# u's products over four token tiles at a time, GELU stores a piece later, two more x tiles kept in DRAM

## The chip, the cores and the metric

One NeuronCore of a Trainium2 chip runs the kernel. The metric is device microseconds of one execution; the kernel before has a median of 753.14 us over three runs (752.85 to 754.17).

## The reference

With x of 2048 tokens by D = 640, the output is a gated mix of two layers.

```python
g = sigmoid((x * gate_w).sum(-1))
a = Re(DFT_seq @ (x @ DFT_hid))          # Cr @ (x Dr^T) - Ci @ (x Di^T)
q = x @ w_q                               # 32 heads x 2 halves of 128
s1, s2 = q1 @ k1.T, q2 @ k2.T             # 16 keys each
top_e, top_s = best 2 of the 4 sums of the best 2 of s1 and of s2
act = gelu(x @ u[top_e])                  # u: 256 experts x 640
b = sum over heads and k of softmax(top_s) * act * v[top_e]
out = g * a + (1 - g) * b
```

All 256 products x @ u.T are computed for every token, and the chosen ones are weighted afterwards. "u's products" are these: 256 experts by 2048 tokens, contracted over 640, then GELU.

## The kernel before

Every product is made in a three-matmul form: both operands are split into a high and a low part (a ScalarE copy makes the high part, a subtraction on VectorE or GpSimd the low one), and `mm3` (L141) issues high x high, high x low and low x high into one accumulator bank.

**Pieces.** The backbone is `seq_piece(n)` (L229) for n = 0 to 127: the product of one 128 x 512 piece of the sequence DFT with one x tile, 5 x 3 matmuls of 512 columns into banks 0 to 4. 16 pieces make a piece sum q, which ScalarE copies into the five buffers ST (L246), VectorE multiplies by the gate (`gate_piece`) and a DMA stores (`store_piece`, L221, on ScalarE's queue). A piece's data is loaded five pieces ahead and split three pieces ahead (`load_piece`, `split_piece`). After the pieces a tail of 2 x 42 steps multiplies the sums by the hidden DFT and by v.

**The order is written by hand.** `at(n, f)` (L196) hangs f behind piece n; `follow(n)` (L199) runs what hangs there, in the order in which it was hung. "Place 24" below is what hangs behind piece 24. Each engine and each DMA queue (SP's, ScalarE's, GpSimd's) executes its share of this one order in sequence and waits at the first thing that isn't ready. VectorE's search for the best keys (`topk`, `gates`, `weights`) comes in small portions: `run_bg` gives them a credit for each TensorE stretch, so they are spread over the pieces. `weights` (L669) is a batch of four tiles' softmax, `put_rows` (L695) copies its transposed rows on ScalarE (L697).

**First phase, pieces 0 to 29.** All 16 x tiles are split and kept in SBUF (X0 to X15). Beside the pieces, `w_part` (L358) multiplies w_q with the keys in eight groups G, at places 6, 9, ..., 27: 32 matmuls (L365) on four tiles of wq (`load_wq`, 640 KB each, five buffers, on SP's queue, at the places between). `make_t` forms sums of the results. As later stages need the space, `put_x` (L449) stores X0 to X8 to DRAM (AWAY = 9) at places 6 to 22; `get_x` (L452) brings tiles back when a later round of 16 pieces needs them, through X6 to X8 in turn. The five stores of piece sum 0 hang at place 24. u is loaded and split at places 21 to 27 (`load_u`, `split_u`), the first token pair's xT at place 26 (`split_xT`, xh on ScalarE, xl on GpSimd), its sums at place 28 (`sum_xT`, L429, VectorE).

**Second phase, pieces 30 to 65.** Beside the pieces run eight score steps p = 0 to 7 (two token tiles each) in four parts a = 0 to 3, one part a place (`score_step`, L544), with one free piece ahead of steps 2, 4 and 6 ("free": nothing of a score step hangs at it). Part 0 multiplies into bank A (two mm3), has ScalarE split four sums of xT (`split_sums_xT`, L443), runs `u_pair` (L720) and copies A to Z on ScalarE (L548). Part 1 goes on in Z (three mm3), copies it out, and makes products Y (bank 6), then Z again. Parts 2 and 3 finish the scores of the two tiles and hang the search for their best keys into the background; part 3 ends with `sum_xT` of the next pair on VectorE. `u_pair(p)` makes u's products of its two tiles: 2 x 5 mm3 with 256 moving columns (two tiles of 128) into bank 7, one GELU of 128 x 512 (L729), and two stores of 128 KB by SP, all within part 0.

**Third phase.** From N1 = 66 on, the background goes on with the search and builds the experts' weights; `load_dd` and `split_dd` bring the hidden DFT. For the tail, buffers of x tiles are lent out again in the order of `raw_tags` (L950).

Of the kernel before, what the change touches and what calls it, by code (L numbers as in the profile page):

```python
# [38 lines left out]
KZ = KD + 1  # L39
NSTEP = 7 * KZ  # L40
AHEAD = 5
AWAY = 9
BYPASS = 4
ACCUM_END = NT * (NC + 2) - 4

# [61 lines left out]
def gated_mix_kernel(ctx: ExitStack, tc: tile.TileContext, xT, xn, dreT, dimT, wsre, wsim, wq, kT, uT, vv, gw, out):  # L107
# [20 lines left out]
    def ps_t(shape, dt=F32):  # L128
        return bank(7, shape, dt)
# [6 lines left out]
    def split(f, h, l, eng):  # L136

        nc.scalar.activation(h, f, AF.Copy)  # L138
        eng.tensor_sub(l, f, h.bitcast(F32))  # L139
# [15 lines left out]
    def run_bg(us):  # L155
        bg.run(us, share)
# [39 lines left out]
    def at(n, f, *args):  # L196
        then.setdefault(n, []).append(lambda: f(*args))
# [51 lines left out]
    for q in range(2 * NC):  # L249
        n = NT * (q + 1)  # L250
        at(n + (2 if q == 0 else -2 if q > 1 else -1), load_row, q)
        at(n + (7 if q == 0 else 0), gate_piece, q)
        if q in (1, 2, 3, 4):
            for d in range(KD):
                at(n + 1 + d, store_piece, q, (d,))
        else:
            at(n + (8 if q == 0 else 1), store_piece, q)


    p1_stack = ctx.enter_context(ExitStack())  # L260
    p1 = p1_stack.enter_context(tc.tile_pool(name="p1", bufs=1, reuse_waits="tile"))
    pools = [p1]

    def load_x(s):
        if s < NT:
# [4 lines left out]
    def split_x(s):  # L270

        if s < NT:
            X[s] = big.tile([P, 2, D], F32R, name="X", tag=f"X{s}")
            f = xr[s // 2][:, s % 2]
            if s:
                split(f, X[s][:, 0], X[s][:, 1], nc.vector)
                return
            psp[0] = h, l = WS[:, 0, 0], WS[:, 0, 1]
            a, b, w = slice(0, 2 * P), slice(2 * P, D), pf.pop(0)
            nc.vector.tensor_copy(X[0][:, 0, a], f[:, a])  # L280
            nc.scalar.activation(h, w, AF.Copy)
            nc.scalar.activation(X[0][:, 0, b], f[:, b], AF.Copy)
            nc.vector.tensor_sub(l, w, h.bitcast(F32))
            for c in (a, b):
                nc.vector.tensor_sub(X[0][:, 1, c], f[:, c], X[0][:, 0, c].bitcast(F32))
# [20 lines left out]


    warm = nc.const_aps.tensor(1.0, [P, 2 * P], mybir.dt.bfloat16)
    t = ps_t([P, 2 * P])
    for n in range(WARM):  # L310
        nc.tensor.matmul(t, warm[:, :P], warm, start=True, stop=True)  # L311

    split_x(0)
    load_piece(4)
# [105 lines left out]
    def split_xT(p, n):  # L420

        if p < NP:
            if not xs:
                xs.update((t, big.tile([P, 2, KD, P], F32R, name=t, tag=t)) for t in ("xh", "xl"))
            split(xf[p][:, n], xs["xh"][:, n], xs["xl"][:, n], nc.gpsimd)

    SX = {}

# [21 lines left out]
        nc.sync.dma_start(xd[s], X[s].bitcast(F32))  # L450

    def get_x(s, tag):  # L452
        X[s] = big.tile([P, 2, D], F32R, name="X", tag=f"X{tag}")
        nc.sync.dma_start(X[s].bitcast(F32), xd[s])

    for s in range(AWAY):
        at(6 + 2 * s, put_x, s)
    for s in range(3):
        at(2 * NT - 5 + s, get_x, s, 6 + s)
    for n in range(NT - 4):  # L460
        at(n, load_x, n + 4)
    for n in range(NT - 3):
# [6 lines left out]
    for G in range(NG):  # L469
        b = 6 + 3 * G  # L470
        for m in range(4 * G, 4 * G + 4):
            at(b, w_part, m)
        at(b, split_w, G)
        if G >= NG // 2:
            at(b + (4, 3, 2, 1)[G - NG // 2], make_t, G)
        for i, m in enumerate(range(4 * G + WQB, 4 * G + WQB + 4)):
            at(b + i // 2, load_wq, m)
    n = b + 2
    at(n - 8, load_xT, 0)
    for k in range(KD):  # L480
        at(n - 8 + k, load_u, k)
        at(n - 6 + k, split_u, k)
    for a in range(2):
        at(n - 3, split_xT, 0, a)
    at(n - 1, sum_xT, 0)
    assert N0 == n + 1

# [34 lines left out]
    def products(o, *terms, first=False):  # L522


        terms = [t for a, w in terms for t in zip(*a, *w)]
        for n, (ah, al, wh, wl) in enumerate(terms):
            mm3(o, ah, al, wh, wl, first and n == 0, n == len(terms) - 1, True)
            run_bg(0.68)

    def x_part(n, k0, k1):  # L530
        return [[xs[t][:, n, k] for k in range(k0, k1)] for t in ("xh", "xl")]

    def s_part(n):
        return [[t[:, k * P:(k + 1) * P] for k in range(2)] for t in SX[n]]

    def w_part2(k0, k1, c):
        return [[w[:, k, c * TC:(c + 1) * TC] for k in range(k0, k1)] for w in (WH, WL)]

    def t_part(n):
        return [[w[:, k] for k in range(2)] for w in TW[n]]  # L540
# [3 lines left out]
    def score_step(p, a):  # L544


        i0, i1 = 2 * p, 2 * p + 1
        copy = lambda o, f: nc.scalar.activation(o, f, AF.Copy)  # L548
        if a == 0:
            AB["A"] = bank(5)  # L550
            products(AB["A"], (x_part(0, 0, 2), w_part2(0, 2, 0)), first=True)
            split_sums_xT(p)
            u_pair(p)
            AB["Z"] = bank(7)
            copy(AB["Z"], AB["A"])
        elif a == 1:
            products(AB["Z"], (x_part(0, 2, 4), w_part2(2, 4, 0)), (x_part(0, 4, 5), w_part2(4, 5, 0)))
            new_sc(i0)
            copy(sc_half(i0, 0), AB["Z"])
            AB["Y"] = bank(6)  # L560
            products(AB["Y"], (s_part(1), t_part(1)), first=True)
            AB["Z"] = bank(7)
            copy(AB["Z"], AB["Y"])
            load_xT(p + 1)
        elif a == 2:
            products(AB["A"], (s_part(2), t_part(2)))
            copy(sc_half(i0, 1), AB["A"])
            products(AB["Z"], (s_part(4), w_part2(2, 4, 1)), (x_part(0, 4, 5), w_part2(4, 5, 1)))
            nc.vector.tensor_add(sc_half(i0, 1), sc_half(i0, 1), AB["Z"])
            bg.credit -= 0.75  # L570
            picks(i0, scs.pop(i0))
            products(AB["A"], (s_part(3), t_part(3)))
            new_sc(i1)
            copy(sc_half(i1, 1), AB["A"])
            split_xT(p + 1, 0)
        else:
            products(AB["Y"], (x_part(1, 4, 5), w_part2(4, 5, 1)))
            nc.vector.tensor_add(sc_half(i1, 1), sc_half(i1, 1), AB["Y"])
            products(AB["A"], (x_part(1, 2, 4), t_part(4)), (x_part(1, 4, 5), w_part2(4, 5, 0)))
            copy(sc_half(i1, 0), AB["A"])  # L580
            bg.credit -= 0.75
            picks(i1, scs.pop(i1))
            split_xT(p + 1, 1)
            sum_xT(p + 1)
# [132 lines left out]
        if i % NB == NB - 1:  # L717
            bg.add(gates(i // NB))

    def u_pair(p):  # L720
        xh, xl = xs["xh"], xs["xl"]
        ps = bank(7, (P, 2, 2 * P))
        for n in range(2):
            c = slice(n * P, (n + 1) * P)
            for k in range(KD):
                mm3(ps[:, n, :], UH[:, k, c], UL[:, k, c], xh[:, :, k, :], xl[:, :, k, :], k == 0 and n == 0, k == KD - 1, True)
            run_bg(1.8)
        act = p2.tile([P, 2, 2 * P], F32, name="act")
        nc.scalar.activation(act, ps, AF.Gelu_apprx_tanh)  # L729
        for n in range(2):  # L730
            nc.sync.dma_start(actd[n][:, 2 * p * P:2 * (p + 1) * P], act[:, n])

    for p in range(NP):
        n = N0 + 4 * p + p // 2
        for a in range(4):
            at(n + 1 + a, score_step, p, a)
    N1 = n + 5
# [3 lines left out]
            at(n - (3 if s > 2 else 5), get_x, s, 6 + s % 3)  # L741
    for s in range(3, AWAY):
        at(N1 - 5 + s, get_x, s, s)
    for s in range(3):
        at(N1 + 6 + 3 * s, get_x, s, s)

# [116 lines left out]
            draw.pop(m)  # L863

    for m in range(2):
        at(N1 + 4 + 2 * m, load_dd, m)
    for m in range(KD):
        for a in range(2):
            at(N1 + 6 + 5 * m + 2 * a, split_dd, m, a)
# [44 lines left out]
    def split_sums(k):  # L914
        if k == KD:
            f = p3.tile([P, 4 * TC], F32R, name="ts", tag="hot0")
            TS[8] = f[:, :2 * D]
            raw_free.append(f[:, 2 * D:2 * D + TC].bitcast(F32))
            raw_tags.extend((("xf", 2), ("X9", 2)))
        for n in () if k == KD else [k] + ([5 + k // 2] if k % 2 == 0 else []):  # L920
            TS[n] = big.tile([P, 2 * D], F32R, name="ts", tag=f"X{(1, 3, 4, 5, 6, 0, 2, 7)[n]}")
        t = T["t"]
        t1, t5, t3, t6 = (t[:, n * 2 * P:(n + 1) * 2 * P] for n in range(4))
        for n, f in enumerate((t1, t3, t5, t6, t[:, 8 * P:])):
            split(f, t_sum(k, n, 0), t_sum(k, n, 1), nc.gpsimd if n < 2 else nc.vector)
        bg.credit -= 1.0

    def load_v():
        T[KD] = big.tile([P, 2, D], F32, name="dt", tag="X9")
        nc.sync.dma_start(T[KD], vv.rearrange("k p d -> p k d"))  # L930

    def split_v():
# [13 lines left out]
    at(NPC + 14, store_gates, 1)  # L946


    fresh, raw_free = deque(), deque()
    raw_tags = [("X8", 2)] + [("wf", 1)] * 4 + [("X10", 2), ("wf", 1)] + [(f"X{s}", 2) for s in range(11, 16)]  # L950
    raw, sp = {}, {}

    def take(key):
# [305 lines left out]
```

## Time and profile before

| | |
|---|---|
| median of three runs | 753.14 us |
| the profiled execution's own time | 753.44 us |
| its span, first to last instruction | 751.7 us |
| DMA moved | 165.89 MB, mean 221 GB/s |
| granted TensorE clock | 1.0 throughout |

A page of the profile gives each engine's busy time, the span in 40 slices (18.8 us each; a digit is a busy share in tenths), the DMA queues, the chain of work that ended last, the costliest groups and the DMA issues. Views of the trace add the timeline of an engine (start, length, engine, line, operation, output<-inputs, shape, count, and in brackets the idle time before it with what ended it), sums by windows, and the chain in order of time. A matmul's length in the timeline reaches into the next one; the distance between starts is what it costs.

### The profile page before, as it was taken

The numbers are of one execution on the slowest core, as the hardware profiler recorded it, in microseconds if no ns is written. First come the engines' busy times: TensorE is split into PE (matmuls) and PEld (weight loads), VectorE is DVE, ScalarE is ACT, GpSimd is POOL, SyncE is SP. The second block draws the span as 40 slices with busy tenths as digits, with TensorE's granted clock in tenths as the row PEclk, the third lists the DMA queues.
The fourth block names the chain that finished last, engine by engine and source line by source line (L and its number), as shares of the span: only waits on it lengthen the run. The fifth ranks groups of instructions, "written<-read, shape, count | busy, mean of one in ns | idle before, by whom it ended". The sixth has DMA issues, their size and how long they took to land.

```text
span 751.7 us, 11366 instructions
## 1 busy us (share of the span) xinstructions
PE 746.7 (99%) x4045; PEld 610.7 (81%) x4045; DVE 587.4 (78%) x741; ACT 361.7 (48%) x660; POOL 346.6 (46%) x286
## 2 busy tenths in 40 slices
PE   9999999999999999999999999999999999999998
PEld 7777777888888888888888888888888888888887
DVE  6864088278999999998999888979999983357651
ACT  4334134534345835553734687633555653443451
POOL 5533225342424424334345445643356793487253
PEclk9999999999999999999999999999999999999999
DMA  9999999478366786663496856388766689775301
GB/s 334 378 388 356 342 381 345 132 191 278 57 174 149 184 273 164 159 167 118 121 376 210 175 146 203 116 255 291 264 225 209 218 261 335 228 233 182 112 29 71
DMA packets 84490, 165.89 MB, mean 221 GB/s; under 512 B 16081, under 2 KB 23377, under 8 KB 84177
## 3 DMA queue, kind: packets, MB, share of 16 engines
q1 hardware_dynamic: 70960, 140.89, 55.5%
q0 software_dynamic: 5472, 9.96, 8.6%
q10 hardware_dynamic: 8000, 14.31, 5.2%
q8 instruction: 32, 0.52, 0.3%
q14 instruction: 26, 0.20, 0.1%
HBM read 132.46 MB, written 31.08 MB: 218 GB/s over the span
## 4 chain that ended last, share of the span: by engine, by line
PE 96%; DMA 2%; DVE 2%; issue 0%; SPq 0%; ACT 0%
PE b L143 30%; PE b L144 30%; PE b L145 30%; PE b L239 2%; PE b L365 2%; DMA wq<-in_wq 2%; PE b L815 1%; PE b L311 1%; DVE ST L217 1%; DVE WU L139 0%; DVE tw L139 0%; DVE wp L371 0%; ACT WU L138 0%; DVE tt L397 0%; DVE tt L396 0%
## 5 line engine op out<-in xcount | busy, mean ns | idle before, releaser
L143 PE MATMUL b<-WS,X 128*128 128x512 f32 x620 | 243.5, 393 | 0.0
L144 PE MATMUL b<-WS,X 128*128 128x512 f32 x620 | 241.5, 389 | 0.0
L145 PE MATMUL b<-WS,X 128*128 128x512 f32 x620 | 241.3, 389 | 0.0
L139 POOL TENSOR_TENSOR WS<-wf,WS 128x512 fp32r<-128x512 f32 x89 | 135.9, 1532 | 162.8 <-ACT WS L138 157.9
L143 PEld LDWEIGHTS b<-WS,X 128*128 128x128 f32 x620 | 116.4, 188 | 28.0 <-issue 4.1
L145 PEld LDWEIGHTS b<-WS,X 128*128 128x128 f32 x620 | 116.4, 188 | 24.5
L144 PEld LDWEIGHTS b<-WS,X 128*128 128x128 f32 x620 | 116.4, 188 | 23.3
L138 ACT ACTIVATE WS<-wf 128x512 fp32r<-128x512 f32 x89 | 55.7, 629 | 76.9 <-PE b L145 32.1
L803 DVE TENSOR_TENSOR hot<-rows,wtab 128x1024 f16<-128x1024 f16 x64 | 62.7, 1005 | 0.7 <-PE b L815 0.6
L139 POOL TENSOR_TENSOR WS<-ra,WS 128x512 fp32r<-128x512 f32 x39 | 55.1, 1426 | 15.3 <-ACT WS L138 13.2
L139 POOL TENSOR_TENSOR xl<-xf,xh 128x640 fp32r<-128x640 f32 x16 | 28.2, 1767 | 69.3 <-ACT xh L138 62.9
L138 ACT ACTIVATE WS<-ra 128x512 fp32r<-128x512 f32 x55 | 34.5, 631 | 50.9 <-PE b L145 36.0
L548 ACT ACTIVATE sc<-b 128x512 f32<-128x512 f32 x32 | 19.2, 600 | 80.7 <-PE b L145 80.7
L191 POOL DMA_DIRECT2D WS<-in_wsre x30 | 26.4, 880 | 68.0 <-ACT WS L189 66.6
L773 ACT ACTIVATE b<-b,mask 128x128 f32<-128x128 f32 x128 | 43.0, 342 | 13.5 <-PE b L815 10.4
L139 POOL TENSOR_TENSOR WP<-ra,WP 128x512 fp32r<-128x512 f32 x18 | 26.4, 1482 | 43.2 <-ACT WP L138 43.1
L598 DVE TENSOR_TENSOR eq<-sc,mm 128x1024 f16<-128x1024 f32 x32 | 41.4, 1293 | 0.9
L605 DVE TENSOR_REDUCE tied<-eq 128x64 f32<-128x1024 f16 x32 | 39.0, 1219 | 0.9
L596 DVE TENSOR_REDUCE mm<-sc 128x64 f32<-128x1024 f32 x32 | 38.8, 1212 | 0.3
L217 DVE SCALAR_TENSOR_TENSOR ST<-ST,grow 128x512 f32<-128x512 f32 x40 | 31.4, 846 | 0.6 <-ACT ST L246 0.6
L143 PE MATMUL b<-WU,xh 128*128 128x512 f32 x80 | 31.2, 391 | 0.0
L145 PE MATMUL b<-WU,xl 128*128 128x512 f32 x80 | 31.1, 389 | 0.0
(203 smaller groups left out, 1468.8 us busy)
## 6 DMA issues: line engine op xcount, KB each, us to landing
wq<-in_wq SPq DMA_DIRECT2D x32, 640.0 KB, 7.1
X<-xd SPq DMA_DIRECT2D x30, 640.0 KB, 6.6
wf<-in_wsim SPq DMA_DIRECT2D x64, 256.0 KB, 4.8
wf<-in_wsre SPq DMA_DIRECT2D x63, 256.0 KB, 6.5
ra<-pd SPq DMA_DIRECT2D x47, 256.0 KB, 3.7
pd<-ST ACTq DMA_DIRECT2D x35, 256.0 KB, 5.2
WS<-in_wsre POOLq DMA_DIRECT2D x30, 256.0 KB, 5.3
xd<-X SPq DMA_DIRECT2D x9, 640.0 KB, 9.4
```

What stands on the lines that cost most here:

```text
L138: nc.scalar.activation(h, f, AF.Copy)
L139: eng.tensor_sub(l, f, h.bitcast(F32))
L143: nc.tensor.matmul(o, wh, ah, start=first, stop=False, skip_group_check=more)
L144: nc.tensor.matmul(o, wh, al, start=False, stop=False, skip_group_check=more)
L145: nc.tensor.matmul(o, wl, ah, start=False, stop=last, skip_group_check=more)
L191: nc.gpsimd.dma_start(l, (wsre, wsim)[w][c, s], accum_op=OP.add)
L217: nc.vector.scalar_tensor_tensor(f, f, -1.0 if w else 1.0, g, op0=OP.mult, op1=OP.mult)
L596: nc.vector.tensor_reduce(m, sc, op=OP.max, axis=AX.X)
L598: nc.vector.tensor_tensor(eq, sc, m[:, :, None].to_broadcast([P, HH, E]), op=OP.is_equal)
L605: nc.vector.tensor_reduce(tied[:, s, ib, :], eq, op=OP.add, axis=AX.X)
L773: nc.scalar.activation(f[:, :, n], f[:, :, n], AF.Copy, scale=mask4[:, n:n + 1])
L803: nc.vector.tensor_tensor(o, a, b, op=op)
```

## The change

u's products are made once for two score steps, in part 0 of the odd ones: 2 x 5 mm3 with 512 moving columns (four tiles), expert half 0 into bank 7 and half 1 into bank 6. GELU of half 0 follows at once; SP stores it in part 1 (256 KB), where GELU of half 1 follows into the same buffer; that is stored in part 2. For this the split xT of two pairs is kept, in the space of X9 and X10 (xh) and of X11 and X12 (xl). X9 and X10 are therefore stored too (AWAY = 11), at place 25 behind the last load of wq, and come back like the others; X11 and X12 are copied by ScalarE into the old places of xh and xl at places 16 and 17, and back at N1. The free piece stands ahead of steps 1, 3 and 5; N1 stays 66. Piece sum 0 is stored at place 28, the first xT split at place 27, the first two load_dd one and two places later. The last warm-up matmul writes the other half of its bank. In the tail v's raw tile takes the first half of the space of X9 and X10, and what is lent out is cut anew: as many buffers, in another order.

```diff
 AHEAD = 5
-AWAY = 9
+AWAY = 11
 BYPASS = 4
...
         else:
-            at(n + (8 if q == 0 else 1), store_piece, q)
+            at(n + (12 if q == 0 else 1), store_piece, q)
     p1_stack = ctx.enter_context(ExitStack())
...
     pools = [p1]
+    TWIN = {}
+    def place(tag):
+        if tag in (9, 11):
+            TWIN[tag] = big.tile([P, 2, 2, D], F32R, name="X", tag=f"X{tag}")
+        if tag in (9, 10, 11, 12):
+            return TWIN[tag - (tag + 1) % 2][:, (tag + 1) % 2]
+        return big.tile([P, 2, D], F32R, name="X", tag=f"X{tag}" if isinstance(tag, int) else tag)
+    def move_x(s, tag):
+        old, X[s] = X[s], place(tag)
+        nc.scalar.activation(X[s], old.bitcast(F32), AF.Copy)
     def load_x(s):
...
         if s < NT:
-            X[s] = big.tile([P, 2, D], F32R, name="X", tag=f"X{s}")
+            X[s] = place(s)
             f = xr[s // 2][:, s % 2]
...
     warm = nc.const_aps.tensor(1.0, [P, 2 * P], mybir.dt.bfloat16)
-    t = ps_t([P, 2 * P])
+    t = ps_t([P, TC])
     for n in range(WARM):
-        nc.tensor.matmul(t, warm[:, :P], warm, start=True, stop=True)
+        c = slice(0, 2 * P) if n < WARM - 1 else slice(2 * P, TC)
+        nc.tensor.matmul(t[:, c], warm[:, :P], warm, start=n < WARM - 1, stop=True, skip_group_check=n == WARM - 1)
     split_x(0)
...
             if not xs:
-                xs.update((t, big.tile([P, 2, KD, P], F32R, name=t, tag=t)) for t in ("xh", "xl"))
-            split(xf[p][:, n], xs["xh"][:, n], xs["xl"][:, n], nc.gpsimd)
+                xs.update((t, big.tile([P, 2, 2, KD, P], F32R, name=t, tag=tag)) for t, tag in (("xh", "X9"), ("xl", "X11")))
+            split(xf[p][:, n], xs["xh"][:, p % 2, n], xs["xl"][:, p % 2, n], nc.gpsimd)
     SX = {}
...
     def get_x(s, tag):
-        X[s] = big.tile([P, 2, D], F32R, name="X", tag=f"X{tag}")
+        X[s] = place(tag)
         nc.sync.dma_start(X[s].bitcast(F32), xd[s])
-    for s in range(AWAY):
+    for s in range(9):
         at(6 + 2 * s, put_x, s)
...
         at(2 * NT - 5 + s, get_x, s, 6 + s)
+    for s, tag in ((11, "xh"), (12, "xl")):
+        at(s + 5, move_x, s, tag)
     for n in range(NT - 4):
...
             at(b + i // 2, load_wq, m)
+    for s in range(9, AWAY):
+        at(b - 2, put_x, s)
     n = b + 2
...
     for a in range(2):
-        at(n - 3, split_xT, 0, a)
+        at(n - 2, split_xT, 0, a)
     at(n - 1, sum_xT, 0)
...
             run_bg(0.68)
-    def x_part(n, k0, k1):
-        return [[xs[t][:, n, k] for k in range(k0, k1)] for t in ("xh", "xl")]
+    def x_part(p, n, k0, k1):
+        return [[xs[t][:, p % 2, n, k] for k in range(k0, k1)] for t in ("xh", "xl")]
     def s_part(n):
...
             AB["A"] = bank(5)
-            products(AB["A"], (x_part(0, 0, 2), w_part2(0, 2, 0)), first=True)
+            products(AB["A"], (x_part(p, 0, 0, 2), w_part2(0, 2, 0)), first=True)
             split_sums_xT(p)
-            u_pair(p)
+            if p % 2:
+                u_pairs(p // 2)
             AB["Z"] = bank(7)
...
         elif a == 1:
-            products(AB["Z"], (x_part(0, 2, 4), w_part2(2, 4, 0)), (x_part(0, 4, 5), w_part2(4, 5, 0)))
+            if p % 2:
+                store_act(p, 0)
+                put_act(1)
+            products(AB["Z"], (x_part(p, 0, 2, 4), w_part2(2, 4, 0)), (x_part(p, 0, 4, 5), w_part2(4, 5, 0)))
             new_sc(i0)
...
         elif a == 2:
+            if p % 2:
+                store_act(p, 1)
             products(AB["A"], (s_part(2), t_part(2)))
             copy(sc_half(i0, 1), AB["A"])
-            products(AB["Z"], (s_part(4), w_part2(2, 4, 1)), (x_part(0, 4, 5), w_part2(4, 5, 1)))
+            products(AB["Z"], (s_part(4), w_part2(2, 4, 1)), (x_part(p, 0, 4, 5), w_part2(4, 5, 1)))
             nc.vector.tensor_add(sc_half(i0, 1), sc_half(i0, 1), AB["Z"])
...
         else:
-            products(AB["Y"], (x_part(1, 4, 5), w_part2(4, 5, 1)))
+            products(AB["Y"], (x_part(p, 1, 4, 5), w_part2(4, 5, 1)))
             nc.vector.tensor_add(sc_half(i1, 1), sc_half(i1, 1), AB["Y"])
-            products(AB["A"], (x_part(1, 2, 4), t_part(4)), (x_part(1, 4, 5), w_part2(4, 5, 0)))
+            products(AB["A"], (x_part(p, 1, 2, 4), t_part(4)), (x_part(p, 1, 4, 5), w_part2(4, 5, 0)))
             copy(sc_half(i1, 0), AB["A"])
...
             bg.add(gates(i // NB))
-    def u_pair(p):
+    def put_act(n):
+        AB["act"] = f = p2.tile([P, TC], F32, name="act")
+        nc.scalar.activation(f, AB.pop(("u", n)), AF.Gelu_apprx_tanh)
+    def store_act(p, n):
+        nc.sync.dma_start(actd[n][:, p // 2 * TC:(p // 2 + 1) * TC], AB.pop("act"))
+    def u_pairs(c):
         xh, xl = xs["xh"], xs["xl"]
-        ps = bank(7, (P, 2, 2 * P))
         for n in range(2):
-            c = slice(n * P, (n + 1) * P)
+            e = slice(n * P, (n + 1) * P)
+            AB["u", n] = ps = bank(7 - n)
             for k in range(KD):
-                mm3(ps[:, n, :], UH[:, k, c], UL[:, k, c], xh[:, :, k, :], xl[:, :, k, :], k == 0 and n == 0, k == KD - 1, True)
-            run_bg(1.8)
-        act = p2.tile([P, 2, 2 * P], F32, name="act")
-        nc.scalar.activation(act, ps, AF.Gelu_apprx_tanh)
-        for n in range(2):
-            nc.sync.dma_start(actd[n][:, 2 * p * P:2 * (p + 1) * P], act[:, n])
+                mm3(ps, UH[:, k, e], UL[:, k, e], xh[:, :, :, k, :], xl[:, :, :, k, :], k == 0, k == KD - 1)
+                run_bg(0.68)
+            if n == 0:
+                put_act(0)
     for p in range(NP):
-        n = N0 + 4 * p + p // 2
+        n = N0 + 4 * p + min((p + 1) // 2, 3)
         for a in range(4):
...
         at(N1 - 5 + s, get_x, s, s)
+    for s in (11, 12):
+        at(N1, move_x, s, s)
     for s in range(3):
...
     for m in range(2):
-        at(N1 + 4 + 2 * m, load_dd, m)
+        at(N1 + 5 + 3 * m, load_dd, m)
     for m in range(KD):
...
             TS[8] = f[:, :2 * D]
-            raw_free.append(f[:, 2 * D:2 * D + TC].bitcast(F32))
-            raw_tags.extend((("xf", 2), ("X9", 2)))
+            raw_free.extend(LENT[0][:, a * TC:(a + 1) * TC] for a in range(2))
+            raw_tags.append(("xf", 2))
         for n in () if k == KD else [k] + ([5 + k // 2] if k % 2 == 0 else []):
...
     def load_v():
-        T[KD] = big.tile([P, 2, D], F32, name="dt", tag="X9")
+        f = big.tile([P, 2, 2, D], F32, name="dt", tag="X9")
+        T[KD], f = f[:, 0], f[:, 1].rearrange("p k d -> p (k d)")
+        fresh.extend(f[:, a * TC:(a + 1) * TC] for a in range(2))
+        LENT.append(T[KD].rearrange("p k d -> p (k d)"))
         nc.sync.dma_start(T[KD], vv.rearrange("k p d -> p k d"))
...
     at(NPC + 14, store_gates, 1)
-    fresh, raw_free = deque(), deque()
-    raw_tags = [("X8", 2)] + [("wf", 1)] * 4 + [("X10", 2), ("wf", 1)] + [(f"X{s}", 2) for s in range(11, 16)]
+    LENT, fresh, raw_free = [], deque(), deque()
+    raw_tags = [("X8", 2)] + [("wf", 1)] * 5 + [("X11", 5)] + [(f"X{s}", 2) for s in range(13, 16)]
     raw, sp = {}, {}
     def take(key):
```

## The prediction

> **What bounds the kernel now.** I read the page's busy shares and chain first, then TensorE's timeline in the three places that the change touches.
>
> ```profile
> PE 746.7 (99%) x4045; PEld 610.7 (81%) x4045; DVE 587.4 (78%) x741; ACT 361.7 (48%) x660; POOL 346.6 (46%) x286
> PE 96%; DMA 2%; DVE 2%; issue 0%; SPq 0%; ACT 0%
> DMA  9999999478366786663496856388766689775301
> ```
>
> TensorE is busy for 99% of the span and holds 96% of the chain that ended last, so the time is the number of matmuls times their spacing, plus the few places where TensorE stands still. The third line says where else to look: the DMA engines are full for the first seven slices of 18.8 us (to about 131 us), which is the first phase and the wq loads, and have room after that.
>
> The spacing, from TensorE's timeline (start, length, line): first a stretch of 512-column matmuls, then the first u_pair.
>
> ```profile
> 125.16 0.39 PE L145 MATMUL b<-WS,X 128*128 128x512 f32 x1
> ...
> 135.36 0.39 PE L145 MATMUL b<-WS,X 128*128 128x512 f32 x1
> ...
> 136.95 0.28 PE L143 MATMUL b<-xh,WU 128*128 128x256 f32 x1
> ...
> 140.54 0.40 PE L143 MATMUL b<-WS,X 128*128 128x512 f32 x1
> ```
>
> Lines come in threes (L143, L144, L145). 45 starts lie between the first two rows: 10.20 / 45 = 0.2267 us for 512 columns. From the third to the fourth row are the 2 x 5 x 3 = 30 matmuls of one u_pair: 3.59 / 30 = 0.1197 us for 256 columns. Two narrow ones take 0.2393 us, one wide one 0.2267: 12.7 ns more. Lengths (0.39, 0.28) overlap and say nothing here; starts do.
>
> The standing still, from TensorE's timeline at the last three w_part blocks (places 21, 24, 27; 32 matmuls each), with what SP's and ScalarE's queues issue near them, and the chain of waits:
>
> ```profile
> 92.85 2.36 PE L365 MATMUL b<-wq,kp 128*32 128x320 f32 x32
> 95.14 0.50 PE L143 MATMUL b<-WS,X 128*128 128x512 f32 x1
> ...
> 105.56 1.82 PE L365 MATMUL b<-wq,kp 128*32 128x320 f32 x24
> 107.61 0.75 PE L365 MATMUL b<-wq,kp 128*32 128x320 f32 x8 [0.22 <-DMA wq<-in_wq]
> 108.28 0.50 PE L143 MATMUL b<-WS,X 128*128 128x512 f32 x1
> ...
> 118.72 1.82 PE L365 MATMUL b<-wq,kp 128*32 128x320 f32 x24
> 121.17 0.74 PE L365 MATMUL b<-wq,kp 128*32 128x320 f32 x8 [0.63 <-DMA wq<-in_wq]
> 121.85 0.50 PE L143 MATMUL b<-WS,X 128*128 128x512 f32 x1
> ```
> ```profile
> 104.64 3.93 ACTq L227 DMA_DIRECT2D pd<-ST  x5
> ```
> ```profile
> 114.24 6.88 DMA wq<-in_wq
> ```
>
> The undisturbed block takes 95.14 - 92.85 = 2.29 us, the next 2.72, the last 3.13: TensorE waits 0.43 + 0.84 = 1.27 us for the last wq tile of each. Just then ScalarE's queue puts out the five stores of piece sum 0 (L227, place 24), and the last load is 6.88 us on its way.
>
> **The change part by part.**
>
> *u's products.* 8 x 30 = 240 narrow matmuls become 4 x 30 = 120 wide ones: 240 x 0.1197 = 28.7 us becomes 120 x 0.2267 = 27.2 us, all of it on TensorE's path: **-1.5 us**. The wide form with four runs of 128 columns (four token tiles) isn't in the trace; the nearest rows are the narrow one with two runs and the wide ones with one run of 512. The narrow one already streams its runs at full rate: 0.2267 - 0.1197 = 0.1070 us for 256 more columns, and twice that is 0.214, so both forms are columns at one rate plus some 13 ns each. Bounds: 0 (the wide form costs two narrow ones) to -1.5; I take -1.5. [...]
>
> *Stores in the full stage.* Its load, by windows (fields: TensorE, weight load, VectorE, ScalarE, GpSimd, clock, DMA share, GB/s), and DMA issues by line (count, KB, us to landing):
>
> ```profile
> 105.00:121.00 16.00, 15.32 (x104) 10.07 (x102) 13.90 (x30) 7.81 (x18) 5.52 (x4) 1.00 1.00 353
> 121.00:131.00 10.00, 9.83 (x48) 7.76 (x49) 8.45 (x15) 4.01 (x10) 6.27 (x5) 1.00 0.90 349
> 131.00:135.00 4.00, 4.00 (x19) 3.30 (x19) 3.33 (x6) 2.53 (x5) 2.42 (x3) 1.00 0.02 6
> ```
> ```profile
> xd<-X SPq DMA_DIRECT2D x9, 640.0 KB, 9.4
> pd<-ST ACTq DMA_DIRECT2D x35, 256.0 KB, 5.2
> actd<-act SPq DMA_DIRECT2D x16, 128.0 KB, 2.2
> ```
>
> Piece sum 0 (5 x 256 KB = 1.31 MB, 3.7 us of DMA at 353 GB/s) leaves place 24 for place 28. X 9 and 10 (2 x 640 KB, the same 1.31 MB) come in at place 25, on SP's queue behind the last wq load, so no wq load stands behind them. The two waits lose 3.7 us of competing traffic against 0.43 and 0.84 us of lateness. Bounds: 0 to **-1.27 us**; I take -1.27. What stands behind the two stores: u's last tile, pieces 31 and 32 and three X loads, 3.7 us later. Who needs them first:
>
> ```profile
> 122.97 0.40 ACT L138 ACTIVATE WU<-uf 128x256 fp32r<-128x256 f32 x1
> ...
> 133.64 2.75 ACT L246 ACTIVATE ST<-b 128x512 f32<-128x512 f32 x5
> ```
> ```profile
> L139 POOL TENSOR_TENSOR WS<-wf,WS 128x512 fp32r<-128x512 f32 x89 | 135.9, 1532 | 162.8 <-ACT WS L138 157.9
> ```
> ```profile
> 119.99 3.08 POOL L139 TENSOR_TENSOR xl<-xf,xh 128x640 fp32r<-128x640 f32 x2 [2.73 <-ACT xh L138]
> ```
>
> The first split of xT now waits (ScalarE, place 27) until the stores have read X 9 and 10. Issued at 114.9 (114.24 plus the load's issue), with 9.4 us to land they are done at 124.3; ScalarE comes there at 122.97 + 0.40 = 123.4. Held 0.9 us, it then makes xh twice, GpSimd xl twice (3.08 us) and the low part of piece 31 (1.53 us), done near 129.5. TensorE wants that in piece 31, whose last matmul starts at 135.36 and its first 14 x 0.2267 earlier, at 132.2, less 1.27: over 1 us of cover. Piece sum 0 issued near 127 lands by 133 in a stage that was empty (131 to 135: 6 GB/s); the next copies into those buffers start at 133.64. Cost 0, or up to 1.5 us if the cover goes.
>
> *Order of the steps.* The free piece now stands ahead of steps 1, 3 and 5, u in the odd steps only. So in steps 2, 4, 6 only one piece (15 x 0.2267 = 3.40 us) lies between the last matmul into A and the first into Z, where u's 3.59 us lay too; in that time ScalarE must split four sums and copy A to Z. Their record, from steps 3, 5 and 7, which have no free piece today (TensorE's first u row, right after A; ScalarE's last sums; its copy):
>
> ```profile
> 228.73 0.28 PE L143 MATMUL b<-xh,WU 128*128 128x256 f32 x1
> 291.05 0.28 PE L143 MATMUL b<-xh,WU 128*128 128x256 f32 x1
> 353.37 0.28 PE L143 MATMUL b<-xh,WU 128*128 128x256 f32 x1
> ```
> ```profile
> 231.40 0.73 ACT L138 ACTIVATE h<-xf 128x256 fp32r<-128x256 f32 x2 [0.46 <-DVE xf L440]
> 291.97 0.72 ACT L138 ACTIVATE h<-xf 128x256 fp32r<-128x256 f32 x2 [0.47 <-DVE xf L440]
> 357.22 0.72 ACT L138 ACTIVATE h<-xf 128x256 fp32r<-128x256 f32 x2 [0.46 <-DVE xf L440]
> 359.89 0.58 ACT L548 ACTIVATE b<-b 128x512 f32<-128x512 f32 x1
> ```
>
> Sums' end plus 0.58 comes 3.98, 2.21 and 5.15 us after A. Against 3.40 us that is late by 0.6, nothing and 1.75. The two late ones follow a batch's gate weights on VectorE, right ahead of xT's sums; and ScalarE has a row copy in it now and then:
>
> ```profile
> 225.71 1.54 DVE L673 TENSOR_TENSOR cc<-cc 128x128 f32<-128x128 f32 x1
> 351.80 1.28 DVE L673 TENSOR_TENSOR cc<-cc 128x128 f32<-128x128 f32 x1
> ```
> ```profile
> 320.55 1.94 ACT L697 ACTIVATE rows<-rt 128x384 f16<-128x384 f16 x1
> ```
>
> A batch closes with an odd step, and its weights come out a step and a half later (batch 0 closes with step 1 and shows at 225.71, just ahead of step 3's A). Steps 2, 4, 6 come right behind the closing step, and behind a long one (free piece and 6.8 us of u), in which VectorE catches up; so step 5 is the nearer row. Bounds 0 to +5.3 us (3 x 1.75). A row copy ahead of the sums takes 2.21 to 4.15 us, 0.75 late; once in three steps, partly inside a wait of ScalarE: I take **+0.5**.
>
> *Step 7* today stalls in the same way:
>
> ```profile
> 360.16 0.39 PE L145 MATMUL b<-WS,X 128*128 128x512 f32 x1
> 360.52 0.50 PE L143 MATMUL b<-WU,xh 128*128 128x512 f32 x1
> 360.86 0.40 PE L144 MATMUL b<-WU,xh 128*128 128x512 f32 x1
> ```
>
> 0.36 + 0.34 against 2 x 0.2267: 0.25 us, for the copy at 359.89. With u doubled 6.8 us lie there instead of 3.6: **-0.25**.
>
> *GELU and its stores.* Eight GELUs stay eight of one size. The second now waits for the store of the first, one buffer, and products Y wait for it, as it reads their bank; behind it on ScalarE are the next copies and splits. On the clock from A's end, with GELU at 0.6 like the copy of its size: half of u 3.40, GELU 0.6, store 2.2 to 5.2 (the rows of 128 and 256 KB), GELU 0.6: 9.8 us at most, wanted after 6.80 + 3.40 + nine matmuls 2.04 = 12.2. In step 7 GELU ends only with the copy's start at 359.89, 6.5 us after A, and the sum is 12.3. So 0. SP reaches the store after the next piece's load, which waits for nothing late; today's SP waits for GELU inside the step, so nothing gets worse there.
>
> *The rest.* Four ScalarE copies of 128x1280 (estimated 1.5 us each: 1280/512 of 0.58) stand where splits run three pieces ahead, 10 us: 0. Six more X loads fall where the DMA has room: 0. Load_dd later, and the tail's buffers in another order with as many of them: 0; if load_v's later slot held the split ahead of the tail, that runs four pieces early. The warm-up's last matmul moves to other columns: 0.
>
> **Sum.** -1.5 - 1.27 + 0.5 - 0.25 = -2.5 us. The profiled execution took 753.44 us (span 751.7), 0.30 above the median 753.14. 753.44 - 2.5 = 750.9 for such an execution; from the median, 750.6.
>
> **The rivals.**
>
> *The wq waits stay* (the lateness of the load's issue decides, not traffic, or other loads fill the gap). For: it is issued at 114.24, only 4.5 us ahead of the block that reads it (118.72). Against: 6.88 us of flight in a full stage, longer than 4.5 by more than the wait. Then -1.5 - 0.25 + 0.5: 751.9, no change by the bound of 0.2% (1.5 us), which is what a measurement here can tell.
>
> *The start of phase two waits* for X 9 and 10's stores by way of xh, GpSimd and piece 31's low part. It decides if they land after about 125.5; 1.5 us later than that costs as much: 752.1.
>
> *The even steps are late, and it gets slower.* If the gate weights or row copies fall ahead of the sums of steps 2, 4 and 6 as in step 7 today, each costs 1.75 us; it decides once the sums end over 2.8 us after A. -3.0 + 5.3: 755.4. VectorE's load speaks for it, the longer odd step against.
>
> *The wide matmul costs two narrow ones*, because the extra goes with the runs and not with the instruction: -1.27 - 0.25 + 0.5: 752.1. The one-run and two-run rows with the same 13 ns speak against it. [...]
>
> **How the numbers follow.** Forecast 0.62 (750.6, own range 749.8 to 751.4); waits stay 0.15; phase two waits 0.09; even steps late 0.09; wide matmul 0.05. The range goes from 749.8 to the third and fifth case, 752.3; outside are the even steps and what is below. Faster by over 0.2% (below 751.6): the forecast, 0.62. Same: 0.15 + 0.09 + 0.05 = 0.29. Slower: 0.09.
>
> **What would show it.** Right: 120 matmuls of 128x512 from UH and UL 0.227 us apart; w_part blocks of 2.29 us at places 24 and 27; no start over 0.3 us late after the even steps' copy of A. Wrong: a gap ahead of Z in steps 2, 4, 6, of piece 31's second matmul, or of Y in odd steps; a wide spacing near 0.239; a DMA wait left at L365.

## The result, and the profile after

The changed kernel takes 764.92 us (median of 5 runs, 762.51 to 766.10) where the kernel before takes 753.14 on the same chip: a ratio of 1.0151, interval 1.0129 to 1.0173. It is 11.8 us slower; the forecast was 750.6. The profiled execution took 764.39 us, with a span of 762.5. One execution of a later experiment (the first of the narrow form, 1938 us, its matmuls of 512 columns 0.62 us apart) is left out of its figures below, since the other nine lie within 752.08 to 754.13.

The page of the changed kernel, busy shares and the DMA slices of 19.1 us:

```profile
PE 748.4 (98%) x3925; PEld 606.1 (79%) x3925; DVE 591.7 (78%) x741; ACT 365.5 (48%) x664; POOL 345.3 (45%) x286
DMA  9999999886755586845199857288866779775301
```

There are 120 matmuls fewer, as the change says, but TensorE's busy time rises by 1.7 us: behind a stall, below, 11 matmuls of 512 columns keep it busy for 4.02 us, where elsewhere 18 fill 4.05. The DMA engines are full in the first seven slices as they were, so wq's loads still run in a full stage. What TensorE waited for, in total, with the count and the longest:

```profile
PE b L143 <- ACT act L747: 8.9, 3, 4.0
PE b L380 <- DMA wq<-in_wq: 1.1, 2, 0.7
```

The second line was there before; the first is new, and L747 is the GELU. Three times TensorE waits for it, and TensorE's timeline shows where: in steps 3, 5 and 7, between the last matmul into Z and the first of products Y (`b<-tw`).

```profile
239.96 0.39 PE L145 MATMUL b<-WU,xl 128*128 128x512 f32 x1
243.48 0.66 PE L143 MATMUL b<-tw 128*128 128x512 f32 x1 [3.13 <-ACT act L747]
243.93 0.63 PE L144 MATMUL b<-tw 128*128 128x512 f32 x1
244.36 0.63 PE L145 MATMUL b<-tw 128*128 128x512 f32 x1
...
306.88 0.39 PE L145 MATMUL b<-WU,xl 128*128 128x512 f32 x1
311.29 0.50 PE L143 MATMUL b<-tw 128*128 128x512 f32 x1 [4.02 <-ACT act L747]
...
371.27 0.39 PE L145 MATMUL b<-WU,xl 128*128 128x512 f32 x1
373.45 0.50 PE L143 MATMUL b<-tw 128*128 128x512 f32 x1 [1.79 <-ACT act L747]
373.79 0.39 PE L144 MATMUL b<-tw 128*128 128x512 f32 x1
```

Start to start, less the usual 0.2267, the stalls are 3.29, 4.18 and 1.95 us. The rows at 243.93 and 244.36 show a second cost: after the first stall matmuls start 0.43 us apart. The windows behind the first and the third stall (TensorE, weight load, VectorE, ScalarE, GpSimd, granted clock, DMA share, GB/s):

```profile
243.48:247.50 4.02, 4.02 (x11) 3.16 (x12) 3.48 (x4) 1.55 (x3) 0.00 (x0) 0.58 0.51 166
373.45:377.50 4.05, 4.05 (x18) 3.35 (x19) 3.95 (x5) 1.56 (x3) 1.10 (x1) 1.00 0.30 92
```

Over the 4 us after the first stall the granted clock averages 0.58, and 11 matmuls run where 18 run after the third. The same follows the second stall (0.59). Summed over the starts, the three places cost 5.04, 5.91 and 2.09 us: **13.0 us**, of which 9.4 are standing still and 3.6 the slow matmuls and the restarts behind them.

Why GELU is late, in step 3: the two GELUs on ScalarE, then SP's queue, then VectorE's last row ahead of SP's transpose.

```profile
231.55 0.60 ACT L747 ACTIVATE act<-b 128x512 f32<-128x512 f32 x1 [1.20 <-PE b L145]
...
242.83 0.60 ACT L747 ACTIVATE act<-b 128x512 f32<-128x512 f32 x1 [8.87 <-DMA actd<-act]
```
```profile
221.40 1.17 SPq L717 DMA_TRANSPOSE rt<-rp  x1
232.72 1.09 SPq L717 DMA_TRANSPOSE rt<-gs  x1
233.87 0.57 SPq L469 DMA_DIRECT2D X<-xd  x1
234.55 0.37 SPq L177 DMA_DIRECT2D wf<-in_wsre  x1
234.97 0.42 SPq L210 DMA_DIRECT2D grow<-gdr  x1
235.48 0.38 SPq L750 DMA_DIRECT2D actd<-act  x1
```
```profile
232.27 0.43 DVE L701 TENSOR_TENSOR gs<-cc,gs 128x256 f16<-128x256 f32 x1
```

GELU of half 0 ends at 232.15. Its store hangs a place later, so in SP's order it stands behind the background's transposes of the chosen rows and gate weights (L717). From 222.6 to 232.72 SP does nothing: it holds the transpose of `gs`, which VectorE finishes at 232.27 + 0.43 = 232.70. Then SP puts out all that has gathered, X, wf and the gate row (640 + 256 + 256 KB), and only then the store, 3.3 us after GELU. The store takes 7.3 us to land, and GELU of half 1 needs that one buffer: it starts at 242.83. TensorE was ready for products Y at 240.19. In step 5 the transpose is let go at 302.48 and the store issued at 305.65 (GELU was done at 299.07), in step 7 at 369.21 and 370.40 (done at 366.04); they land after 4.9 and 2.4 us, behind 896 and 0 KB of such loads. In step 1 no batch of weights exists yet, and nothing stalls.

SP is held in the same way in the kernel before, but no store is late for it. In step 3, on SP's queue and on ScalarE:

```profile
228.07 1.09 SPq L692 DMA_TRANSPOSE rt<-gs  x1
234.06 0.82 SPq L731 DMA_DIRECT2D actd<-act  x2
```
```profile
233.44 0.60 ACT L729 ACTIVATE act<-b 128x512 f32<-128x512 f32 x1
```

There the transpose is let go 6 us before GELU ends, and the stores go out 0.02 us behind GELU, as they do within 0.03 us in all eight steps. In the kernel before VectorE has the gate weights done 6.0, 0.3 and 6.0 us before GELU's end in steps 3, 5 and 7; in the changed kernel they come 0.6, 3.4 and 3.1 us after the end of GELU of half 0. So the change did two things at once: it hung the store behind the transposes, and it moved the event that the transposes wait for behind GELU.

### The profile page after: what moved, and what is told of

Read it like the earlier page. It is cut to its first block, busy times and chain, and to the rows that moved or that the text cites. A ratio compares the mean times of both kernels' runs of the same rounds, so it can differ in the third digit from the quotient of the medians.

```text
span 762.5 us, 11141 instructions
## 1 busy us (share of the span) xinstructions
PE 748.4 (98%) x3925; PEld 606.1 (79%) x3925; DVE 591.7 (78%) x741; ACT 365.5 (48%) x664; POOL 345.3 (45%) x286
## 4 chain that ended last, share of the span: by engine, by line
PE 67%; issue 15%; POOL 6%; DMA 5%; DVE 5%; ACT 0%; POOLq 0%; DVEq 0%; SPq 0%
PE b L143 21%; PE b L144 21%; PE b L145 21%; DMA wq<-in_wq 3%; POOL WS L191 2%; POOL xl L139 2%; PE b L239 2%; DMA xr<-in_xn 2%; POOL tw L139 2%; PE b L380 1%; PE b L850 1%; DVE eq L623 1%; DMA gdr<-gc 1%; DVE tied L630 1%; DVE mm L621 1%
## 5 line engine op out<-in xcount | busy, mean ns | idle before, releaser
L838 DVE TENSOR_TENSOR hot<-rows,wtab 128x1024 f16<-128x1024 f16 x64 | 57.3, 921 | 2.6 <-PE b L850 2.6
L139 POOL TENSOR_TENSOR WS<-ra,WS 128x512 fp32r<-128x512 f32 x33 | 46.7, 1424 | 14.4 <-ACT WS L138 14.2
L138 ACT ACTIVATE WS<-ra 128x512 fp32r<-128x512 f32 x47 | 29.4, 631 | 42.4 <-PE b L145 31.0
L217 DVE SCALAR_TENSOR_TENSOR ST<-ST,grow 128x512 f32<-128x512 f32 x40 | 34.4, 919 | 1.2 <-ACT h L138 1.2
L139 POOL TENSOR_TENSOR WP<-ra,WP 128x512 fp32r<-128x512 f32 x13 | 19.0, 1470 | 31.3 <-ACT WP L138 31.2
L838 DVE TENSOR_TENSOR hot<-hot,rows 128x1024 f16<-128x1024 f16 x32 | 31.4, 983 | 0.0
```

The source lines that it names most:

```text
L217: nc.vector.scalar_tensor_tensor(f, f, -1.0 if w else 1.0, g, op0=OP.mult, op1=OP.mult)
L838: nc.vector.tensor_tensor(o, a, b, op=op)
```

## The experiments

**Theory 1**: the store of half 0, hung a piece later, comes behind SP's held transposes and the loads that they held up; through one buffer it holds GELU of half 1, and so products Y. **Theory 2**: GELU of half 1, in bank 6 and on ScalarE, is late by itself. **Theory 3**: the store's landing time is at fault, not its place. The median of one and the same kernel differs by up to 1 us from one set of executions to the next (753.08 to 754.09 for the kernel before), so each ratio is to the kernel before on the same chip.

### Two buffers

```diff
-        AB["act"] = f = p2.tile([P, TC], F32, name="act")
+        AB["act"] = f = p2.tile([P, TC], F32, name="act", bufs=2)
```

(Four small constants moved to another pool and one tile shared another's space, to make room.)

> The changed kernel with two buffers for GELU's result instead of one, so that the second GELU does not wait for the store of the first (room for it: four small tables move to the first phase's pool, and one small tile shares the space of another). Theory 1 (one buffer, and its store late on SP's queue): the three waits ahead of products Y and the slow matmuls behind two of them go, 5.0 + 5.9 + 2.1 = 13.0 us in the profile of the changed kernel, so 764.9 - 13.0 = 751.9 us. Theory 2 (the second GELU is late because ScalarE itself is late, or the sharing of bank 6 is what costs): the waits stay, 762 to 766 us.

Measured: 750.42 us (750.19 to 751.57), ratio 0.9952 (0.9936 to 0.9969). The timelines of ScalarE and SP in step 3:

```profile
230.36 0.60 ACT L748 ACTIVATE act<-b 128x512 f32<-128x512 f32 x1 [1.20 <-PE b L145]
...
233.76 0.60 ACT L748 ACTIVATE act<-b 128x512 f32<-128x512 f32 x1 [0.98 <-PE b L145]
```
```profile
231.54 1.09 SPq L718 DMA_TRANSPOSE rt<-gs  x1
...
234.30 0.38 SPq L751 DMA_DIRECT2D actd<-act  x1
```

The store is as late as before (GELU done at 230.96, store at 234.30; landing up to 9.4 us), and nobody waits for it: GELU of half 1 follows as soon as TensorE has made its sums. Theory 2 falls, and a store issued 3.3 us after its GELU is seen to cost nothing where nobody waits for its buffer. That the time is 1.5 us under the 751.9 expected fits the waits for wq: they are 1.7 us in the changed kernel's profile, which that sum kept, and 0.1 in this one.

### The store on ScalarE's queue

```diff
-        nc.sync.dma_start(actd[n][:, p // 2 * TC:(p // 2 + 1) * TC], AB.pop("act"))
+        nc.scalar.dma_start(actd[n][:, p // 2 * TC:(p // 2 + 1) * TC], AB.pop("act"))
```

> The changed kernel with GELU's stores issued by ScalarE's queue instead of SP's, one buffer as before. Theory 1 with SP's queue as the larger part: the store goes out about 2 us after the GELU instead of 3.3, 6.6 and 4.4 us, and lands in 2.2 to 4 us; no wait is left in step 7 and at most 0.5 us in steps 3 and 5: 752 to 753 us. Theory 3 (the landing is the larger part, 7.3 us in step 3 and 5.0 in step 5): 1 to 2 us of waiting stay in steps 3 and 5: 754 to 757 us. Theory 2: 762 to 766 us.

Measured: 768.90 us (766.25 to 771.40), ratio 1.0192 (1.0162 to 1.0221). Away from SP's queue it got worse, which no theory expected. ScalarE's timeline in step 3:

```profile
230.60 0.60 ACT L747 ACTIVATE act<-b 128x512 f32<-128x512 f32 x1 [1.21 <-PE b L145]
...
241.51 0.33 ACTq L750 DMA_DIRECT2D actd<-act  x1
244.43 0.60 ACT L747 ACTIVATE act<-b 128x512 f32<-128x512 f32 x1 [11.41 <-DMA actd<-act]
```

It landed quickly (2.4 to 4.2 us) but was issued 10.3 us after its GELU. The store waits not for GELU alone: it signals its end by a semaphore (a counter; in the trace one instruction raises it and another waits for it) that a transpose of `gs` on SP's queue uses too, and goes out only when that has landed. The trace has number 108 at both. The transpose is issued at 237.18 and lands 4.3 us later, at 241.48, and the store goes out at 241.51; in steps 5 and 7, with numbers 110 and 100, the transposes land at 307.79 and 372.91 and the stores go out at 307.80 and 372.93. So it still stands behind SP's transposes, and ScalarE itself is now held with it. A store with a semaphore of its own wasn't run.

### The store back behind its GELU

```diff
         elif a == 1:
             if p % 2:
-                store_act(p, 0)
                 put_act(1)
...
             if n == 0:
                 put_act(0)
+                store_act(2 * c + 1, 0)
```

> The changed kernel with the store of GELU half 0 put back into part 0, right behind its GELU, still by SP and with one buffer; in SP's order it now stands ahead of the transposes of the rows in step 3. Theory 1: the store goes out as soon as the GELU is done and the waits go: 751.9 us, up to 753 if the transposes still stand ahead of it in one of the steps. Theory 3: with 5 to 7 us of landing GELU half 1 is ready about when products Y want it: 752 to 754 us. Theory 2: 762 to 766 us.

Measured: 749.89 us (749.75 to 749.98), ratio 0.9940 (0.9925 to 0.9955). SP's queue in step 3:

```profile
230.47 0.33 SPq L749 DMA_DIRECT2D actd<-act  x1
230.89 2.48 SPq L716 DMA_TRANSPOSE rt<-rp  x2
```

Here SP reaches the store first, and the transposes follow. All of the loss is undone by one line at its old place, with one buffer and everything else of the change kept. Its median here is the lowest of all runs. The same kernel ran twice more: 750.05 us (749.56 to 751.72; 0.9958, 0.9942 to 0.9974) and 750.80 (750.01 to 751.77; 0.9962, 0.9950 to 0.9974).

> The kernel with the first store back behind its GELU once more, unchanged, so that the other three have it beside them on the same chip: 749.9 us, and its waits for wq show how far they wander between executions.

> The kernel with the first store back behind its GELU, unchanged, beside the two others on the same chip: 749.9 to 750.1 us.

### The transposes later, the store where the change puts it

```diff
-            bg.space(lambda a=a: step(a), 5.0 if a else 16.0 if b == NT // NB - 1 else 8.0)
+            bg.space(lambda a=a: step(a), 5.0 if a else 16.0)
```

> The changed kernel with the transposes of a batch's rows hung 16 us instead of 8 us behind the batch's weights, so that SP meets them when VectorE has the weights done. GELU's stores as in the change. Theory 1 (SP is held by the first transpose, which waits for VectorE): the stores go out on time, 752 to 754 us. If only the place in the queue counts and not the wait for VectorE, part of the waits stays: 755 to 760 us. Theory 2: 762 to 766 us.

Measured: 751.51 us (750.99 to 752.22), ratio 0.9964 (0.9951 to 0.9977). The store, still a piece late, is issued at 230.76, 0.02 us after GELU; ScalarE waits 1.1 us once for a store, and TensorE never for GELU. The price is elsewhere, on TensorE's timeline of this kernel: the experts' weights come later too.

```profile
420.69 0.44 PE L850 MATMUL b<-hot 128*64 128x64 f16 x16 [0.92 <-DVE hot L838]
```

So "a piece later" is no fault in itself; what stands ahead in SP's order, and has to wait there, is.

### The store a place later in the kernel before

```diff
         elif a == 1:
+            store_act(p)
             products(AB["Z"], (x_part(0, 2, 4), w_part2(2, 4, 0)), (x_part(0, 4, 5), w_part2(4, 5, 0)))
```

(The two stores are taken out of `u_pair`.)

> The kernel before with one part of the change alone: the two stores of each GELU result hang in part 1, one piece later, still on SP's queue and still from one buffer. By my theory lateness alone costs nothing, since here the next GELU into that buffer comes a whole step later: 753.1 to 753.6, no gap ahead of products Y. If a store behind the rows' transposes disturbs by itself (their landing, or the X loads behind it), some of the 13 us shows here: 755 or more.

Measured: 753.19 us (752.77 to 754.80), ratio 0.9998 (0.9986 to 1.0010): nothing. But no store is late in this kernel either. Step 3 on ScalarE and on SP's queue:

```profile
232.75 0.60 ACT L730 ACTIVATE act<-b 128x512 f32<-128x512 f32 x1
```
```profile
233.37 0.80 SPq L736 DMA_DIRECT2D actd<-act  x2
```

All eight pairs of stores go out 0.02 to 0.03 us behind their GELU, since SP's transposes were let go before (at 227.38 in step 3) or stand behind the stores (in step 5). So hanging a store a place later makes it late only where the queue is held past GELU's end, and this run says nothing of what a late store costs. That it takes both, a late store and a reader of its buffer within the same step, rests on two other runs: two buffers (late, no wait) and the store back behind its GELU (one buffer, not late).

### Behind the transposes, but ahead of the loads

```diff
             copy(AB["Z"], AB["A"])
+            if p % 2:
+                store_act(p, 0)
         elif a == 1:
             if p % 2:
-                store_act(p, 0)
                 put_act(1)
```

> The changed kernel, one buffer, with the store of half 0 hung at the end of part 0. In steps 3 and 5 it then still stands behind the transposes that wait for VectorE, but ahead of the loads of X, wf and the gate row that follow them (1152 KB and 896 KB); in step 7 ahead of the transposes. In the changed kernel the store took 7.3, 5.0 and 2.4 us to land behind 1152, 896 and 0 KB. If those loads ahead of it made the slow landing: issued near 233.9 and 304.5, landed 2.4 us later, GELU of half 1 done near 236.9 and 307.5 where products Y want it at 240.2 and 307.1: no stall in steps 3 and 7, at most 0.4 us in step 5, 749.9 to 750.8 in all. If the held issue alone is enough, and the landing stays at 7.3 and 5.0: stalls of 1.6 and 3.0 us in steps 3 and 5, 754 to 757.

Measured: 751.33 us (750.75 to 752.29), ratio 0.9975 (0.9966 to 0.9985), 0.5 us above the range expected, with 0.8 us of waits for wq in its profile. SP's queue in step 3, and TensorE's timeline in step 5:

```profile
232.60 1.10 SPq L718 DMA_TRANSPOSE rt<-gs  x1
233.79 0.53 SPq L751 DMA_DIRECT2D actd<-act  x1
234.38 0.42 SPq L469 DMA_DIRECT2D X<-xd  x1
```
```profile
302.72 0.50 PE L143 MATMUL b<-tw 128*128 128x512 f32 x1 [0.50 <-ACT act L748]
```

SP is held as long as before, until 232.60. But the store goes out first and lands in 2.7 us (3.8 in step 5), not 7.3 (4.9). Step 3 doesn't stall, step 5 by 0.8 us, without a slow stretch. Theory 3 is half right: the landing is what makes a late issue costly, and the landing is slow because the loads that the same wait held up go out ahead of the store.

### u's products in narrow matmuls

The store is back behind its GELU in this kernel and the next two.

```diff
-                mm3(ps, UH[:, k, e], UL[:, k, e], xh[:, :, :, k, :], xl[:, :, :, k, :], k == 0, k == KD - 1)
+                for j in range(2):
+                    o = ps[:, 2 * j * P:2 * (j + 1) * P]
+                    mm3(o, UH[:, k, e], UL[:, k, e], xh[:, j, :, k, :], xl[:, j, :, k, :], k == 0 and j == 0, k == KD - 1, True)
```

> As the kernel with the first store back behind its GELU (749.9 us), but each wide matmul of u's products is cut into two of 256 columns, 240 in place of 120, in the same places. If the wide form is worth what the spacing of starts says (240 x 0.1197 against 120 x 0.2267), this is 1.5 us slower: 751.4, starts 0.120 us apart. If the wide form is worth nothing by itself and the gain came from elsewhere: 749.9.

> The kernel with u's products in two matmuls of 256 columns once more. It came out 2.7 us above the kernel it is made from, where the spacing of starts says 1.5. If 1.5 is right: starts 0.120 us apart, no gap in the odd steps, and 1.5 us over the unchanged kernel beside it, the rest being waits for wq. If the narrow form costs more: a spacing over 0.120, or a gap at one of the 40 places where the weights change.

Measured: 752.62 us (752.08 to 754.13), 2.6 over the unchanged kernel beside it (the one with the store back behind its GELU), ratio to the kernel before 0.9987 (0.9975 to 0.9999); again 752.92 (752.07 to 753.91; 0.9987, 0.9977 to 0.9998), 2.1 over. Step 3 on TensorE's timeline of the second, its 60 narrow matmuls and what follows:

```profile
227.52 0.28 PE L143 MATMUL b<-xh,WU 128*128 128x256 f32 x1
...
234.71 0.40 PE L143 MATMUL b<-WS,X 128*128 128x512 f32 x1
```

and the 30 wide ones of the changed kernel:

```profile
227.95 0.39 PE L143 MATMUL b<-xh,WU 128*128 128x512 f32 x1
...
234.75 0.39 PE L143 MATMUL b<-WS,X 128*128 128x512 f32 x1
```

7.19 against 6.80 us, four times: 1.56 us, and no gap beside. What the medians show above that is within what the waits for wq vary by.

### Piece sum 0 stored at place 24 again

```diff
-            at(n + (12 if q == 0 else 1), store_piece, q)
+            at(n + (8 if q == 0 else 1), store_piece, q)
```

> As the kernel with the first store back behind its GELU (749.9 us), but the five stores of piece sum 0 back at place 24. If that traffic made the last two waits for wq, they return, 0.4 to 1.3 us: 750.3 to 751.2, with w_part blocks of 2.7 and 3.1 us at places 24 and 27. If these waits wander from execution to execution whatever is stored there: 749.9, blocks of 2.3 to 2.4 us, or a late block at some other place.

Measured: 751.72 us (750.58 to 752.41), ratio 0.9972 (0.9962 to 0.9983), 1.7 over the unchanged kernel beside it. Its last w_part block on TensorE's timeline:

```profile
117.78 1.82 PE L380 MATMUL b<-wq,kp 128*32 128x320 f32 x24
121.19 0.75 PE L380 MATMUL b<-wq,kp 128*32 128x320 f32 x8 [1.59 <-DMA wq<-in_wq]
```

The wait at place 27 is back, with 1.8 us. But the waits also wander: summed over the eight blocks, above 2.29 us each, they are 0.09, 0.60 and 1.89 us in the three profiles of the very same unchanged kernel. One profile decides nothing here. The median is 0.9 to 1.8 us above the three of the unchanged kernel, and all profiles together agree: with the stores of piece sum 0 at place 24 (this run, the kernel before, that with its store hung later) the block at place 27 is 0.84, 1.34 and 1.80 us long beyond 2.29, with them at place 28 (ten profiles) 0 to 0.68. The sum over the eight blocks is 1.5 us on average with place 24, 0.6 with place 28.

### The free piece ahead of steps 2, 4 and 6 again

```diff
-        n = N0 + 4 * p + min((p + 1) // 2, 3)
+        n = N0 + 4 * p + p // 2
```

> As the kernel with the first store back behind its GELU (749.9 us), but the free piece again ahead of steps 2, 4 and 6. The steps with u's products then follow the step before them at once. If the order of the steps costs nothing, as the missing gaps in steps 2, 4 and 6 say: 749.9. If the odd steps need the free piece ahead of them: a gap of 0.3 to 1.8 us ahead of products Z in each of steps 3, 5 and 7, up to 755.2.

Measured: 750.77 us (749.51 to 751.96), ratio 0.9966 (0.9951 to 0.9981), and no gap in any score step on TensorE's timeline. The order of the steps costs nothing either way.

### All spans on one footing

Taking from each profiled span its waits for wq, its late starts in the first 9 us and the stalls of TensorE named above leaves the matmuls and what always goes with them: 762.5 - 1.73 - 0.14 - 13.04 = 747.6 us for the changed kernel, 747.6 to 747.9 for the eight profiles of the experiments that kept the wide form on SP's queue, and 749.4 to 749.7 for the kernel before, for that with its store hung later and for the narrow form. So the wide form is worth 1.5 to 2.1 us in the changed kernel too, and the stalls account for its loss.

## Why the prediction was wrong

It said 750.6 us, faster. It failed at one step, which it costed at nothing.

- **GELU and its stores: 0, measured +13.0.** The working allowed, from A's end, half of u, GELU, 2.2 to 5.2 us for the store, GELU: "9.8 us at most, wanted after ... 12.2". In step 3, counted from u's first matmul at 227.95, products Y were wanted after 12.2 us indeed, but GELU of half 1 ended after 15.5. Three things were missed. The store's issue was taken to follow GELU, since "SP reaches the store after the next piece's load, which waits for nothing late": the queue was listed from the code of pieces and score steps, and the transposes that the background puts into the same queue were left out. They, and the loads let go with them, cost 3.3, 6.6 and 4.4 us from GELU's end to the issue in steps 3, 5 and 7. The landing was bounded by the median of other stores (5.2), where it was 7.3 behind 1152 KB released with it. And the two stalls of over 3 us cost 3.5 us more by the clock, a price in no part of the sum. Even without these the working left no room in step 7: its own upper sum there, 12.3, was past the 12.2 at which the result was wanted, and still it put 0.
- The prediction had half of the fact in hand: it quoted a batch's weights "just ahead of step 3's A" as a risk to VectorE's sums, and didn't ask which queue waits for these weights, nor whether they still come before GELU's end once the change has moved both. They don't: 0.6 to 3.4 us after it, where they came 0.3 to 6.0 before. What moved them wasn't separated; with the free piece back at its old places they still come 0.5, 3.4 and 0.5 us after. Among its signs of being wrong the prediction did list a gap ahead of products Y in the odd steps.
- **u's products: -1.5, right.** 6.80 us for 30 wide matmuls against 7.19 for 60 narrow ones: -1.56.
- **Waits for wq: -1.27, right in direction and about right in size.** Undoing that move costs 0.9 to 1.8 us in the medians, and 0.9 us on average in the profiles. In the profile of the changed kernel the late blocks are at places 12 and 18, 1.7 us in all, so the mark set for it (blocks of 2.29 at places 24 and 27) is met at place 24 only.
- **Even steps: +0.5, measured 0.** Steps 2, 4 and 6 show no gap, with the free piece in either place.
- **Step 7: -0.25, right**: the gap at the copy is gone, and another in its place.
- **The rest: 0, right.** No wait at the start of phase two, none in the tail.

With the store back behind its GELU, the sum is -1.5 - 1.27 - 0.25 = -3.0 us; measured were 4.2, 3.6 and 3.0 us less than the kernel before on the same chip (749.9, 750.1 and 750.8 us). That these come close to the 750.6 of the forecast doesn't save it: they are times of another kernel. None of the rivals was the one that came; that named for the slow side looked for its 5.3 us in the even steps, the true one was in the odd steps, in a queue.

## What to carry to other kernels

Before an instruction is moved down a queue, list everything that will stand ahead of it there, the background's issues too, and ask of each what it waits for: in step 3 one transpose, held for VectorE until 232.72, kept 1152 KB of loads and the store behind it and let them go in one burst, so the store was issued 3.3 us after its GELU and then took 7.3 us to land. With a second buffer a store as late cost nothing (ratio 0.9952 in place of 1.0151): count buffers together with places. And ask of a change that gathers work into fewer, larger bursts whether what a queue waits for still comes before what stands behind it: here it came 0.3 to 6.0 us before, and then 0.6 to 3.4 us after.

## What the runs showed of the hardware

- **A stall can cost more than itself.** After idle times of 3.13 and 4.02 us of TensorE the granted clock was 0.50 for 3.41 us, from 243.67 and from 311.93 on (0.2 and 0.6 us behind the restart), and matmuls of 512 columns started 0.427 us apart instead of 0.2267, 1.7 us lost each time; after 1.79 and 0.50 us it stayed at 1.0. But in the kernel with its store on ScalarE's queue, an idle time of 3.13 us as well was followed by a granted clock of 1.0 and starts 0.23 us apart:

```profile
376.29 0.50 PE L143 MATMUL b<-tw 128*128 128x512 f32 x1 [3.13 <-ACT act L747]
376.62 0.39 PE L144 MATMUL b<-tw 128*128 128x512 f32 x1
376.86 0.40 PE L145 MATMUL b<-tw 128*128 128x512 f32 x1
```

  So the length of a stall alone didn't tell what followed: of two idle times of 3.13 us one was followed by 0.50 and one by 1.0. What else decides wasn't shown.
- **Another queue is not always another order**: a store on ScalarE's queue went out 10.3 us after its GELU, 0.03 us behind the landing of a transpose of SP's with which it shared a semaphore.
